# A new hand-written step order for a fused linear-attention and feed-forward kernel

## The chip, the cores and the metric

One core of a Trainium2 chip runs the whole kernel. The metric is the device time of one execution in microseconds. Before the change it is 151.06 us, the median of three runs (150.97 to 152.73).

The core has five engines that run side by side, each with its own queue of instructions that it works off strictly in order: TensorE (PE: matmuls, with PEld for loading weights into its array), VectorE (DVE), ScalarE (ACT), GpSimd (POOL) and SyncE (SP, which here only issues DMAs; ACT issues a few as well). Engines wait for each other through semaphores. An instruction that waits holds up everything behind it on its own engine.

## The reference, cut to what matters

```
xn  = layernorm(x)                                   # x: 2048 rows of 448, bf16
q, k, v = split(xn @ wqkv)                           # 16 heads of 28
phi(a)  = concat(softmax(a @ w_phi), softmax(-a @ w_phi))     # per head, 28 -> 56
kv = phi(k)^T v ;  z = sum of phi(k) over the rows   # over all 2048 rows
o  = (phi(q) kv) / (phi(q) z + 1e-6)
h  = xn @ w1 + b1                                    # 448 -> 1792
out = x + o @ wo + (h * tanh(softplus(h))) @ w2      # Mish in the middle
```

Because kv and z are sums over all rows, no row of the attention output can be made before every row's k and v have been.

## The kernel before, in words

**Tiling.** The 2048 rows are 16 tiles of 128 (t = 0 to 15), worked on in 8 pairs (u = 0 to 7, tiles 2u and 2u+1). Everything in bf16 stays in SBUF. PSUM is eight banks, used as four pairs of banks; a pair of row tiles or a feed-forward step holds one such bank pair from its first matmul until its result has been moved out.

**Where the order comes from.** There is no loop nest that decides the order. Every piece of work is a named step, a closure in a dictionary `steps`, and one string, `ORDER` (L147 on), lists the 298 names; `run_order` calls them one after the other:

```
def run_order(steps, order):
    for name in order:
        steps[name]()
```

Calling a step appends its instructions to the queues of the engines that it uses, so `ORDER` fixes the order within each of the five queues at once, and also which bank each step gets (the least recently used free one). Waits between engines are worked out from what each instruction reads and writes. Most steps exist in variants; the last letter says which engine does the work.

**The steps by name** (u a pair, t a tile, c a chunk of 128 rows of a weight):

- `lx0 lx1 lx2 lx3 lx4 lx6` load x: tiles 0-1, 2-3, 4-5, 6-7, 8-11, 12-15 (L270). `lkm`, `lvm` load the first 384 rows of the k and v weights, `lkt` their last 64 rows, twice (L273, L281). `lqT0..3` load the q weights transposed (L285). `lp`, `lb`, `lo`, `l2` load w_phi, b1, wo, w2; `l1m0..2` load chunks of W1 (L277), `l1t` its last 64 rows, twice (L281). A final `s` means issued by SP, `a` by ACT. `table` loads the ACT table for exp and ln (L315).
- `pi pm pw pv pk pp0 pp1 pp2` are set-up work on POOL (identity, masks, zeros, ones); `bd` builds the block-diagonal w_phi (L544). `z12` is twelve 128x512 matmuls on constants whose result nobody reads (L376).
- `st{t}` layernorm statistics of a tile: `d` on DVE (BATCH_NORM_STATS2 and an aggregate, L467, L468), `a` on ACT (copy with a sum, a small multiply, square with a sum). `rs{u}` makes 1/sqrt(var): `p` on POOL (L473, L476), `a` on ACT for both tiles at once, `t` on ACT tile by tile (L480, L482). `xn{u}` normalizes a pair: `d` on DVE (L501), `p` on POOL (L496) after a small DVE step (L489).
- `xt{u}` transposes the normalized pair into `xnT`: `m` by a DMA transpose that SP issues (L521), `a` or `d` by seven PE transposes (L509) moved out of PSUM by ACT or DVE, `b` the same with the move split, three blocks on ACT and four on DVE. A DMA transpose (but for pair 1) also waits for the loads of the first and the last tiles of x.
- `wtk{c}`, `wmk{c}`, `wmq{c}` fold w_phi into the k and q weights: PE transposes of the k weights (L556), then 112-row matmuls (L571); the last letter is the engine that moves the result out (L514 on ACT, L516 on DVE).
- `v{u}1 v{u}2`, `k{u}1 k{u}2`, `q{u}1 q{u}2` are the projections of a pair, each in two parts of 8 and 6 matmuls (L438) which work in the two 64-row halves of the array side by side. After part 2 of k and q, ACT makes the two exponentials (L600, L661); v is moved out by ACT (`a`) or DVE (`d`).
- `kn{u}.{s}` normalizes phi(k): a row sum and a reciprocal on DVE (L608, L610), the multiplication on POOL (L612). `kv{u}` adds a pair to kv and z on PE (L629). `kvz` moves kv out on DVE (L641) and transposes it by DMA.
- `e{t}` transposes phi(q) of a tile by DMA (L669). `nd{t}` makes numerator and denominator on PE (L703) and divides on DVE (L718 to L729). `ot{u}m` transposes the attention output by DMA (L738).
- `f{q}.{fc}{part}` is the first feed-forward matmul for half the rows (q = 0, 1) and 128 of the 1792 features (L438, 64x512 operands), in parts of 8 and 6 matmuls, then Mish on ACT (L680).
- `wo{u}`, `G{u}` and `g{t}` add the two output products (L843, L805, L821), DVE adds x (L770), `sto`, `stt` store (L861, L858).

**Order around the start in the queues before.** SP: lx3, lkm, lkt, lx2, lqT2, lqT1, lqT0, lqT3, lx6, lx0, lx4, l1t, xt2m, l1m2, l1m0, xt7m, ... PE: z12, wtk2, wtk0, wtk1, wmk2, xt3, wtk3, wmk0, wmk1, wmk3, v31, b1, v32, k31, ... ACT: lp, table, lx1, lb, lvm, rs3, the moves of wtk2 and wtk1, ...

Of the kernel before, what the change touches and what calls it, by code (L numbers as in the profile page):

```python
# [144 lines left out]


ORDER = """  # L147
lpa pp2 lx3s pm z12 st6d pi lkms table st7d pw lx1a lkts lba lvma bd rs3t wtk2a xn3d lx2s lqT2 wtk0d st3d pv wtk1a wmk2a
xt3a wtk3d lqT1 wmk0a wmk1a st2d wmk3a st5d v31d rs1p lqT0 st4d xn1d rs2p lqT3 b1 qd lx6s v32a k31 lx0s wmq1a lx4s pp1
wmq0a xn2p l1ts xt1d st14d st15d wmq2a wmq3a k32 k11 st12d rs7p st9d q11 xt2m st8d k12 st10d xn7d q31 rs4p v11d pp0 q12  # L150
xn4p st11d v12d q21 rs5p st13d q32 q22 xn5p k21 st0d l1m2s l1m0s rs6p xt7m v21d k22 st1d v22a ep e3 rs0p v71a pk xt4m
k71 v72a kn3.1 xn6d k72 xt5m k41 xn0d kn3.0 e2 xt6m xt0m v41d e5 k42 l1m1s v42d e4 q41 v51d q42 e6 e8 v52a kn2.0 k61
v61d k62 kn4.0 k01 k51 kn7.0 kn4.1 k02 v62d q51 k52 q52 kn0.0 e7 q61 e9 v01d q62 e12 kn1.1 kn6.1 e10 f0.11 e11 kn1.0
v02d f0.12 kn0.1 f1.01 f0.21 f1.02 f1.21 kn7.1 f1.31 f1.22 los kn2.1 q71 f1.32 f1.51 kn5.0 f0.22 e13 f1.52 q01 q72 q02
f0.61 l2s kn6.0 kv3 kv1 e15 kv2 kn5.1 kv4 kv6 e14 kv7 kv0 kv5 kvz f0.62 f0.71 f0.91 f1.81 f0.72 e1 f1.82 f0.121 f1.111
f0.122 f0.81 f0.92 f1.112 f0.82 f1.91 f0.131 f1.92 e0 nd2 f0.132 f0.31 f0.101 f0.32 nd0 f0.111 f0.102 f0.112 nd1 f1.71
f1.61 f1.72 f0.51 nd3 f1.62 f0.52 f1.41 f1.11 f0.01 f1.12 f0.41 f1.42 ot0m nd5 f0.42 f0.02 wo01 f1.131 f1.101 ot1m nd6
f1.132 G01 nd4 f1.102 G11 ot2m wob nd7 ot3m G02 wo02 f1.121 nd12 G12 f1.122 wo11 nd11 wo22 G31 wo31 nd10 wo12 G21 nd13
ot5m ot6m wo21 wo32 G62 nd8 G22 wo52 G32 nd9 ot4m wo61 G51 nd15 G61 nd14 wo51 G41 wo62 sto6 sto1 wo41 G52 ot7m g14 sto5
wo7F sto2 G42 wo7H sto0 wo42 g15 stt14 sto3 sto4 stt15  # L160
"""


# [824 lines left out]
```

## Time and profile before

| what | value |
| --- | --- |
| median of three runs | 151.06 us (150.97, 151.06, 152.73) |
| the profiled execution's own time | 150.35 us |
| its span, first to last instruction | 148.3 us |
| mean granted TensorE clock | 0.999 |
| busy: DVE, ACT, POOL | 100.7, 72.0, 44.4 us |
| HBM read, written | 7.02 MB, 1.84 MB |

The profile is one execution. Its span runs from the first to the last instruction; the execution's own time is 2.05 us longer, for what lies around the instructions. Times in a timeline are from the span's start. In a timeline row stand the start, the time to the end of the last instruction, the engine, the line, the operation, output and input, and how many instructions were merged; brackets give the idle time before and what ended it. The ends of matmuls are modelled and contain the latency of the array, so the steady pace of matmuls is read from the distance between starts.

### The profile page before, as it was taken

To read this page: it belongs to the slowest core of one execution; us is meant where nothing else is said; L and a number is where in the kernel's file an instruction comes from. 1 tells how busy PE (TensorE), PEld (TensorE's weight loads), DVE (VectorE), ACT (ScalarE), POOL (GpSimd) and SP (SyncE) were. 2 spreads that over 40 slices of the span, in tenths; PEclk is the share of its full clock that TensorE was granted. 3 is DMA by queue.
4 is the path that set the end of the run, shared out by engine and by line. 5 is a ranking of instruction groups with operands and counts; after the bars stand their busy time and mean duration, and the time that the engine had idled before them with its cause. 6 is when DMAs were issued, how large, how long until landed. Compare 5 with 4: busy or idle time off the path is not lost.

```text
span 148.3 us, 3988 instructions
## 1 busy us (share of the span) xinstructions
PE 143.7 (97%) x1731; PEld 75.9 (51%) x1731; DVE 100.7 (68%) x225; ACT 72.0 (49%) x83; POOL 44.4 (30%) x65
## 2 busy tenths in 40 slices
PE   7799999999999999999999999999999999999993
PEld 2456456556555475444454445555555555554452
DVE  0888889897999803003998278896789859983042
ACT  3589889978996899578566653202000000000000
POOL 5428489899899990000000000000000000000000
PEclk9999999999999999999999999999999999999999
DMA  5999998999939989960003300031003300306513
GB/s 123 301 190 346 182 275 130 163 205 256 139 67 174 242 242 267 210 113 0 0 4 62 62 4 0 21 73 34 4 2 66 62 0 4 62 4 186 186 52 134
DMA packets 39997, 17.24 MB, mean 116 GB/s; under 512 B 33964, under 2 KB 39212, under 8 KB 39980
## 3 DMA queue, kind: packets, MB, share of 16 engines
q1 hardware_dynamic: 38800, 16.29, 52.5%
q10 hardware_dynamic: 1180, 0.70, 1.9%
q8 instruction: 13, 0.21, 0.6%
q14 instruction: 4, 0.03, 0.1%
HBM read 7.02 MB, written 1.84 MB: 60 GB/s over the span
## 4 chain that ended last, share of the span: by engine, by line
PE 89%; DMA 6%; DVE 2%; issue 0%; ACT 0%; SPq 0%
PE PS L438 47%; PE PS L843 31%; PE PS L805 3%; DMA Wkv<-in_A_wqkv_dram 3%; DMA xnT<-xn 3%; PE PS L703 2%; PE PS L629 2%; PE PS L571 1%; PE PS L821 1%; DVE stats L467 1%; PE PS L556 1%; PE PS L509 1%; DVE xnT L516 0%; ACT Eq L514 0%; DVE x_all L770 0%
## 5 line engine op out<-in xcount | busy, mean ns | idle before, releaser
L438 PE MATMUL PS<-xnT,W 64*128 64x512 bf16 x392 | 44.8, 376 | 0.0
L680 ACT ACTIVATE actT<-PS,b1T 128x1024 bf16<-128x1024 f32 x28 | 30.1, 1112 | 24.3 <-PE PS L438 24.3
L843 PE MATMUL PS<-W,actT 64*128 64x448 bf16 x392 | 39.3, 349 | 0.0
L438 PEld LDWEIGHTS PS<-xnT,W 64*128 64x128 bf16 x392 | 18.8, 94 | 20.8 <-ACT actT L680 0.5
L843 PEld LDWEIGHTS PS<-W,actT 64*128 64x128 bf16 x392 | 18.1, 94 | 18.1 <-issue 0.3
L612 POOL TENSOR_TENSOR actT<-actT,rSk 128x896 bf16<-128x896 bf16 x16 | 26.6, 1702 | 0.7 <-DVE rSk L610 0.6
L770 DVE TENSOR_TENSOR x_all<-PS,x_all 128x448 bf16<-128x448 f32 (+1 forms) x16 | 9.2, 616 | 11.3 <-PE PS L821 5.6
L718 DVE COPY Sq<-PS 128x16 f32<-128x16 f32 x32 | 4.1, 169 | 18.6 <-PE PS L703 18.5
L608 DVE TENSOR_REDUCE Sk<-actT 128x32 f32<-128x896 bf16 x16 | 16.7, 1043 | 0.0
L600 ACT ACTIVATE actT<-PS 128x896 bf16<-128x896 f32 x16 | 13.8, 950 | 1.0 <-PE PS L438 0.9
L438 PE MATMUL PS<-Wkv,xnT 64*128 64x448 bf16 x112 | 13.2, 349 | 0.0
L438 PE MATMUL PS<-Wpq,xnT 64*128 64x448 bf16 x112 | 12.5, 349 | 0.4 <-DMA xnT<-xn 0.4
L467 DVE BATCH_NORM_STATS2 stats<-x_all 128x6 f32<-128x448 bf16 x16 | 9.7, 608 | 4.1 <-DMA x_all<-in_A_x_dram 4.1
L438 PE MATMUL PS<-Wpk,xnT 64*128 64x448 bf16 x112 | 12.5, 349 | 0.0
L726 DVE TENSOR_TENSOR v_all<-v_all 128x464 f32<-128x464 f32 x16 | 10.3, 642 | 0.6
L722 DVE TENSOR_TENSOR v_all<-PS,Sq 128x464 f32<-128x464 f32 x16 | 10.3, 642 | 0.5
L729 DVE TENSOR_TENSOR xn<-v_all,rden 128x448 bf16<-128x448 f32 x16 | 10.0, 625 | 0.6
L724 DVE TENSOR_TENSOR v_all<-PS,Sq 128x464 f32<-128x464 f32 x16 | 10.1, 631 | 0.0
L661 ACT ACTIVATE actT<-PS 128x896 bf16<-128x896 f32 x10 | 8.6, 921 | 1.1 <-PE PS L438 1.1
L438 PEld LDWEIGHTS PS<-Wpq,xnT 64*128 64x128 bf16 x112 | 5.9, 94 | 5.4 <-issue 0.8
L438 PEld LDWEIGHTS PS<-Wpk,xnT 64*128 64x128 bf16 x112 | 6.0, 94 | 4.4
L438 PEld LDWEIGHTS PS<-Wkv,xnT 64*128 64x128 bf16 x112 | 6.0, 94 | 4.3
(82 smaller groups left out, 126.4 us busy)
## 6 DMA issues: line engine op xcount, KB each, us to landing
W<-in_B_w_dram SPq DMA_DIRECT2D x1, 1568.0 KB, 10.1
out_dram<-x_all SPq DMA_DIRECT2D x7, 224.0 KB, 2.1
W<-in_B_w_dram SPq DMA_DIRECT2D x3, 448.0 KB, 4.1
x_all<-in_A_x_dram SPq DMA_DIRECT2D x2, 448.0 KB, 4.9
x_all<-in_A_x_dram SPq DMA_DIRECT2D x3, 224.0 KB, 3.8
Wo<-in_A_wo_dram SPq DMA_DIRECT2D x2, 336.0 KB, 4.1
W<-in_B_w_dram SPq DMA_DIRECT2D x2, 224.0 KB, 6.4
Wkv<-in_A_wqkv_dram SPq DMA_DIRECT2D x1, 336.0 KB, 4.5
```

The source lines that it names most:

```text
L438: ins = e.matmul(o, lhs(c, k), rhs(c, k), start=part == "1" and c == 0, stop=part == "2" and c == 2)
L467: op("DVE", lambda e: e.bn_stats(stats[:, t, :], x_all[:, t, :]), r=[("x", t)], w=[("st", t)], tag=f"bn{t}")
L600: op("ACT", lambda e, s=s: e.activation(E_of(u)[:, s, :, :], two(b, D), ACT.Exp, scale=1.0 if s == 0 else -1.0), r=[pb(b), pb(b + 1)], w=[ ...
L608: op("DVE", lambda e: e.tensor_reduce(Sk[u][:, s, :], Eh(), AX.X, ALU.add), r=[("E", u, s)], w=[("Sk", u, s)], tag=f"Sk{u}.{s}")
L612: op("POOL", lambda e: e.tensor_tensor(Eh(), Eh(), ap_on(rSk[u][:, s, 0:1], [[1, 2 * H], [0, DH]]), ALU.mult), r=[("E", u, s), ("rSk", u, ...
L680: op("ACT", lambda e: e.activation(actT[:, fc, q * 1024:(q + 1) * 1024], bank(b, 2), ACT.Mish, bias=b1T[:, fc:fc + 1]), r=[("b1T",), pb(b) ...
L722: op("DVE", lambda e: e.tensor_tensor(tv(t1[i]), num(0), sx(1), ALU.mult), r=[pb(b), pb(b + 1), ("Sq", i, 1)], w=[("t1", i)], tag=f"ta{t}")
L724: op("DVE", lambda e: e.tensor_tensor(tv(t2), num(1), sx(0), ALU.mult), r=[pb(b), pb(b + 1), ("Sq", i, 0)], w=[("t2",)], tag=f"tb{t}")
L726: op("DVE", lambda e: e.tensor_tensor(t1[i], t1[i], t2, ALU.add), r=[("t1", i), ("t2",)], w=[("t1", i)], tag=f"tc{t}")
L729: op("DVE", lambda e: e.tensor_tensor(o_sb[(t // 2) % 2][:, t % 2, :].rearrange("p (h d) -> p h d", d=DH), t1[i][:, :, 0:DH], ap_on(rden[i ...
L770: op("DVE", lambda e: e.tensor_tensor(x_all[:, t, 0:n], bank(b)[:, 0:n], x_all[:, t, 0:n], ALU.add), r=[pb(b), ("x", t)], w=[("out", t)], ...
L843: ins = e.matmul(bank(places[par][0])[:, 0:D], l, r, start=fresh[par], stop=places[par][2] and i >= len(todo) - 2)
```

## The change

Only the string `ORDER` changes: the same kernel functions, another sequence and other variants of some steps.

- The loads on SP up to `lx4` keep their queue and their order, and so do those on ACT. The two loads of W1's tail (`l1ts`) go from before `xt2m` to behind `e2`, so that of the loads only Wo and W2 still follow. W2's load goes from SP (`l2s`) to ACT (`l2a`).
- `z12` becomes `z16`: four more matmuls on constants ahead of the first weight transpose.
- On ACT `table` goes behind the four DMA issues. The statistics of tile 7 (`st7`), and 1/sqrt(var) of pairs 0, 1 and 5, go to ACT; pair 3's is made for both tiles at once.
- Pairs 0, 1 and 7 are normalized on POOL, 4 and 5 on DVE (before: 4 and 5 on POOL; 0, 1 and 7 on DVE). The transposes of pairs 1 and 3 are moved out by ACT and DVE together. wtk1 and wmq2 go from ACT to DVE. v is moved out of PSUM by ACT for pairs 1, 3, 4, 5, 6 and by DVE for 0, 2, 7 (before: ACT for 2, 3, 5, 7 and DVE for 0, 1, 4, 6).
- POOL's set-up (`pk`, `pp1`, `pp2`, `pw`) moves ahead of the identity, `pv` behind the last 1/sqrt(var).
- The two multiplications per pair of `kn`, the projections, feed-forward steps and output steps come in a new sequence. In each queue the number of matmuls is the same but for the four constants.

```
-lpa pp2 lx3s pm z12 st6d pi lkms table st7d pw lx1a lkts lba lvma bd rs3t wtk2a xn3d lx2s lqT2 wtk0d st3d pv wtk1a wmk2a
-xt3a wtk3d lqT1 wmk0a wmk1a st2d wmk3a st5d v31d rs1p lqT0 st4d xn1d rs2p lqT3 b1 qd lx6s v32a k31 lx0s wmq1a lx4s pp1
-wmq0a xn2p l1ts xt1d st14d st15d wmq2a wmq3a k32 k11 st12d rs7p st9d q11 xt2m st8d k12 st10d xn7d q31 rs4p v11d pp0 q12
-xn4p st11d v12d q21 rs5p st13d q32 q22 xn5p k21 st0d l1m2s l1m0s rs6p xt7m v21d k22 st1d v22a ep e3 rs0p v71a pk xt4m
-k71 v72a kn3.1 xn6d k72 xt5m k41 xn0d kn3.0 e2 xt6m xt0m v41d e5 k42 l1m1s v42d e4 q41 v51d q42 e6 e8 v52a kn2.0 k61
-v61d k62 kn4.0 k01 k51 kn7.0 kn4.1 k02 v62d q51 k52 q52 kn0.0 e7 q61 e9 v01d q62 e12 kn1.1 kn6.1 e10 f0.11 e11 kn1.0
-v02d f0.12 kn0.1 f1.01 f0.21 f1.02 f1.21 kn7.1 f1.31 f1.22 los kn2.1 q71 f1.32 f1.51 kn5.0 f0.22 e13 f1.52 q01 q72 q02
-f0.61 l2s kn6.0 kv3 kv1 e15 kv2 kn5.1 kv4 kv6 e14 kv7 kv0 kv5 kvz f0.62 f0.71 f0.91 f1.81 f0.72 e1 f1.82 f0.121 f1.111
...
+lpa lx1a lba lvma lx3s lkms lkts lx2s lqT2 lqT1 lqT0 lqT3 lx6s lx0s lx4s pk table pp1 pp2 pw st6d st7a st3d z16 pi st2d
+rs3a xn3d wtk2a wtk0d pm rs1a bd xn1p wtk1d b1 wmk2a xt3b wmk0a wtk3d wmk1a v31a st4d st5d rs2p wmk3a xt1b v32a qd pp0
+xn2p k11 xt2m wmq2d wmq1a st15d st14d ep wmq0a st13d wmq3a rs7p k12 st12d k31 q31 xn7p k32 st1d q32 q11 st9d v11d st8d
+q12 v12a k21 v21d st11d l1m2s xt7m st10d rs4p xn4d rs5a k22 rs6p l1m0s xt4m xn6d pv v22d xn5d q21 kn1.1 st0d k71 q22 k72
+v71a xt6m k41 v72d rs0a xn0p v41a k42 xt5m v42a l1m1s kn7.1 e3 e5 e4 k61 v51a xt0m kn2.1 kn1.0 k62 kn6.0 kn4.0 v52a k51
+e2 q51 l1ts k52 e6 q52 q41 e7 v61a v01a kn3.1 v62a kn3.0 q42 k01 v02d k02 q61 f1.31 q62 kn0.0 f0.11 e9 f1.32 kn0.1 f1.01
+f1.21 f1.02 f1.22 q71 e8 f0.12 q72 q01 kn2.0 e11 e12 f1.51 f0.21 kn7.0 e10 e13 q02 kn5.1 los f1.52 f0.22 kn4.1 kn6.1 kv3
+e1 kv0 kv4 kv2 kv6 kn5.0 kv1 kv7 kv5 kvz f0.31 f1.91 f0.32 f0.51 f0.91 e14 f1.92 f1.81 f0.92 f0.81 f0.52 f0.82 f1.111 e0
+e15 f1.82 f1.11 f1.112 nd1 f1.12 f0.01 nd0 f0.61 f1.71 f0.62 f1.72 l2a f0.111 f0.101 f0.112 f0.02 f0.71 f0.102 nd2 f0.72
+f0.41 nd3 f1.121 wob f0.42 ot0m f0.131 f1.122 f1.101 f0.132 ot1m nd4 f0.121 f1.102 nd5 f1.61 f0.122 f1.62 f1.41 ot2m nd7
+nd6 f1.42 G01 G11 G31 nd13 G02 f1.131 wo01 ot3m wo31 f1.132 G12 wo02 wo32 nd12 wo11 wo22 wo12 G32 nd10 G21 nd11 wo21
+sto3 G61 ot6m ot5m wo61 nd8 G41 nd9 G22 ot4m nd14 sto1 sto2 G62 G51 nd15 sto0 ot7m wo41 wo62 G42 wo51 wo42 wo52 g14 wo7F
+G52 sto4 sto6 wo7H g15 sto5 stt14 stt15
```

More of the change, by code (lines that the diff above doesn't have):

```diff
@@ L153 @@
-v61d k62 kn4.0 k01 k51 kn7.0 kn4.1 k02 v62d q51 k52 q52 kn0.0 e7 q61 e9 v01d q62 e12 kn1.1 kn6.1 e10 f0.11 e11 kn1.0
-v02d f0.12 kn0.1 f1.01 f0.21 f1.02 f1.21 kn7.1 f1.31 f1.22 los kn2.1 q71 f1.32 f1.51 kn5.0 f0.22 e13 f1.52 q01 q72 q02
-f0.61 l2s kn6.0 kv3 kv1 e15 kv2 kn5.1 kv4 kv6 e14 kv7 kv0 kv5 kvz f0.62 f0.71 f0.91 f1.81 f0.72 e1 f1.82 f0.121 f1.111
-f0.122 f0.81 f0.92 f1.112 f0.82 f1.91 f0.131 f1.92 e0 nd2 f0.132 f0.31 f0.101 f0.32 nd0 f0.111 f0.102 f0.112 nd1 f1.71
-f1.61 f1.72 f0.51 nd3 f1.62 f0.52 f1.41 f1.11 f0.01 f1.12 f0.41 f1.42 ot0m nd5 f0.42 f0.02 wo01 f1.131 f1.101 ot1m nd6
@@ L158 @@
-f1.132 G01 nd4 f1.102 G11 ot2m wob nd7 ot3m G02 wo02 f1.121 nd12 G12 f1.122 wo11 nd11 wo22 G31 wo31 nd10 wo12 G21 nd13
-ot5m ot6m wo21 wo32 G62 nd8 G22 wo52 G32 nd9 ot4m wo61 G51 nd15 G61 nd14 wo51 G41 wo62 sto6 sto1 wo41 G52 ot7m g14 sto5
-wo7F sto2 G42 wo7H sto0 wo42 g15 stt14 sto3 sto4 stt15
+lpa lx1a lba lvma lx3s lkms lkts lx2s lqT2 lqT1 lqT0 lqT3 lx6s lx0s lx4s pk table pp1 pp2 pw st6d st7a st3d z16 pi st2d
+rs3a xn3d wtk2a wtk0d pm rs1a bd xn1p wtk1d b1 wmk2a xt3b wmk0a wtk3d wmk1a v31a st4d st5d rs2p wmk3a xt1b v32a qd pp0
```

## The prediction

> **What bounds the kernel now.** I read the stretches first: the span cut where the matmuls change character, with the busy time and count of PE, PEld, DVE, ACT and POOL, then granted clock, DMA share and GB/s.
>
> ```profile
> 0.00:5.94 5.94, 4.65 (x12) 1.61 (x13) 2.09 (x6) 2.28 (x5) 3.54 (x16) 1.00 0.74 189
> 5.94:18.64 12.70, 11.85 (x141) 7.05 (x142) 10.73 (x34) 10.78 (x18) 5.92 (x13) 1.00 1.03 248
> 18.64:53.12 34.48, 34.48 (x351) 19.23 (x352) 30.44 (x57) 30.49 (x34) 32.56 (x34) 1.00 1.01 178
> 53.12:56.38 3.26, 3.26 (x130) 3.18 (x128) 0.00 (x0) 3.25 (x5) 2.42 (x4) 1.00 1.12 335
> 56.38:145.36 88.98, 88.98 (x1093) 44.48 (x1090) 56.67 (x129) 25.15 (x24) 0.00 (x0) 1.00 0.28 62
> 145.36:148.30 2.94, 0.51 (x18) 0.39 (x14) 0.75 (x2) 0.00 (x0) 0.00 (x0) 0.96 0.24 77
> ```
>
> PE is busy for 34.48 of 34.48, 3.26 of 3.26 and 88.98 of 88.98 us: from 18.64 to 145.36, 85% of the span, it has no gap. The change removes none of that work, so it can win only ahead of 18.64 and behind 145.36. The tail of 2.94 us is the last eviction and store, and both orders end in the same steps (half of pair 7's output product, `g15`, the split store). The first 5.94 us wait for k's weights, whose loads keep queue and place. That leaves 5.94 to 18.64, and PE's waits all lie there:
>
> ```profile
> PE PS L556 <- DMA Wkv<-in_A_wqkv_dram: 0.4, 1, 0.4
> PE PS L438 <- DMA xnT<-xn: 0.4, 1, 0.4
> PE PS L571 <- ACT Eq L514: 0.3, 1, 0.3
> ```
>
> They sum to 1.1 us, but ends of matmuls are modelled, so I take the holes from the starts in PE's timeline:
>
> ```profile
> 0.85 4.65 PE L376 MATMUL PS<-const-bfloat16-1.0 128*128 128x512 bf16 x12 [0.85 <-PEq L973]
> 5.94 0.85 PE L556 MATMUL PS<-ident,Wkv 128*112 128x128 bf16 x12 [0.44 <-DMA Wkv<-in_A_wqkv_dram]
> 7.12 0.36 PE L571 MATMUL PS<-Wbd,Eq 112*128 112x112 bf16 x4 [0.33 <-ACT Eq L514]
> 11.49 0.57 PE L571 MATMUL PS<-Wbd,WqT 112*128 112x112 bf16 x8
> 11.89 0.56 PE L509 MATMUL PS<-ident,xn 128*128 128x128 bf16 x7
> 12.29 0.56 PE L571 MATMUL PS<-Wbd,WqT 112*128 112x112 bf16 x8
> 16.95 0.73 PE L438 MATMUL PS<-Wpq,xnT 64*128 64x448 bf16 x6
> 17.52 0.73 PE L438 MATMUL PS<-Wkv,xnT 64*128 64x448 bf16 x6
> 18.64 1.69 PE L438 MATMUL PS<-Wpq,xnT 64*128 64x448 bf16 x16 [0.40 <-DMA xnT<-xn]
> ```
>
> Paces: six projection matmuls go from 16.95 to 17.52 (0.095 each), eight small ones from 11.49 to 11.89 (0.05), seven transposes from 11.89 to 12.29 (0.057). The 141 matmuls of the stretch are 78, 32 and 30 of these and the bias transpose (0.1): 7.4 + 1.6 + 1.7 + 0.1 = 10.8 us in 12.70. So the holes are 1.9 us, and this is the **ceiling of any gain**: 1.3% of the time. One hole is plain: the six from 17.52 need 0.57 too, and the next starts 1.12 later, 0.55 lost to the DMA transpose of pair 2.
>
> **The change, part by part.**
>
> *Warm-up.* Twelve constant matmuls become sixteen. The last rows of that group:
>
> ```profile
> 4.90 0.60 PE L376 MATMUL PS<-const-bfloat16-1.0 128*128 128x512 bf16 x2
> 5.12 0.38 PE L376 MATMUL PS<-const-bfloat16-1.0 128*128 128x512 bf16 x1
> ```
>
> The last two start 0.22 apart. Four more put the last start at 5.12 + 0.88 = 6.00 and free PE at 6.22, where k's weights let it go on at 5.94. Price: +0.28 at that place.
>
> *Early chain.* These rows set it:
>
> ```profile
> 1.27 1.28 ACT L315 ACT_TABLE_LOAD   x1 [1.27 <-PEq L973]
> 1.30 0.48 ACTq L270 DMA_DIRECT2D x_all<-in_A_x_dram  x1
> 2.50 0.41 ACTq L273 DMA_DIRECT2D Wkv<-in_A_wqkv_dram  x1
> 4.61 0.29 ACT L480 ACTIVATE lnv<-mv,eps_col 128x1 f32<-128x1 f32 x1 [2.06 <-DVE mv L468]
> 4.93 0.20 ACT L482 ACTIVATE rstd<-lnv 128x1 f32<-128x1 f32 x1
> 6.38 1.08 ACT L514 ACTIVATE Eq<-PS 112x512 bf16<-112x512 bf16 x2 [0.60 <-PE PS L556]
> x_all<-in_A_x_dram ACTq DMA_DIRECT2D x1, 224.0 KB, 4.1
> 6.60 0.42 DVE L516 COPY Eq<-PS 112x512 bf16<-112x512 bf16 x1 [0.21 <-PE PS L556]
> 10.10 0.60 DVE L467 BATCH_NORM_STATS2 stats<-x_all 128x6 f32<-128x448 bf16 x1
> 10.83 0.86 DVE L501 TENSOR_SCALAR xn<-x_all,mv,rstd 128x448 bf16<-128x448 bf16 x3
> 12.45 1.74 POOL L496 TENSOR_SCALAR xn<-x_all,rstd,shift 128x448 bf16<-128x448 bf16 x3
> ```
>
> The table load runs beside the DMA issues (1.27 and 1.30), so moving it behind them brings x no earlier: tiles 2-3 still land at 1.30 + 4.1 = 5.4. It now runs at 2.9 to 4.2. Then ACT makes tile 7's statistics, which no row shows on ACT. Nearest are a plain move (0.54 each for the two of 512 columns at 6.38) for its two passes over 448 columns and the small 4.61 and 4.93 rows for the multiply: 0.54 + 0.25 + 0.54, about 1.4, which I take; half of that and 2.4 (the passes at double price, for the sum that they carry) are the ends. 1/sqrt(var) adds 0.5 (0.29 + 0.20): ready at 6.1, between 5.4 and 7.1. DVE does tiles 3 and 2 meanwhile (one every 0.73, 10.10 to 10.83): 5.4 to 6.95. So pair 3 is normalized from 6.95 to 7.8 (0.86), and DVE's own statistics hide ACT's; without that cover ACT's upper end would cost 0.15.
>
> PE: wtk2 at 6.22; its eviction and wmk2 as before 1.18 later (5.94 to 7.12), 7.40; xt3 at 7.9, not at 7.3, since DVE is later; wmk0 8.3, wtk3, wmk1 8.85 behind DVE's evictions (0.42 each); v31 at 9.2. POOL normalizes pair 1 in 1.74 from 8.3, so xt1 runs at 10.3. k11 waits for both halves of its eviction, ACT's behind wmk3's and DVE's behind two statistics, until 11.65 (0.4 idle). From there the projections and the four wmq run closed up but for 0.1: k12 ends at 13.9, q31 starts 14.7, v12 ends at **19.27**. Before, the same work and `q32` would be done at 18.64 + 0.57 = 19.21. So 13.27 us from 5.94 become 13.05 from 6.22: 0.28 lost at the start, 0.22 won in holes (0.55 at pair 2's transpose, less 0.33 more in the waits for xt3 and k11): **+0.06 us**. The bounds: -0.9 if the waits for xt3, v31 and k11 (0.35, 0.15, 0.4) are covered; +0.6 if each small DVE and ACT eviction is one 0.42 to 0.54 later.
>
> *W1's tails.* They are two DMAs ahead of pair 2's transpose:
>
> ```profile
> 10.34 1.12 SPq L281 DMA_DIRECT2D W<-in_B_w_dram  x2
> 14.22 1.26 SPq L521 DMA_TRANSPOSE xnT<-xn  x1
> DMA to landing us min/median/max: 3.0/3.5/4.3
> W<-in_B_w_dram SPq DMA_DIRECT2D x2, 224.0 KB, 6.4
> W<-in_B_w_dram SPq DMA_DIRECT2D x1, 1568.0 KB, 10.1
> ```
>
> The issue at 14.22 is POOL's doing (12.45 + 1.74), and POOL is no earlier now. It landed 4.3 later, the slowest of six; without the tails in front it lands 3.0 to 4.3 after issue, 17.2 to 18.5. Both are ahead of 19.27, because `q32` and the rest stand in front of `k21`: the tails' move itself is worth 0 to PE, the new sequence covers the stall either way. The tails now issue behind pair 0's transpose, which POOL releases at 29.9 (below), and `e2`, 1.3 each on SP: 32.6, and at 6.4 they land at 39. The first feed-forward step stands at 19.27 + 16 x 0.76 + 15 x 0.57 = 39.9 (the parts ahead of it). Cover 0.9; should SP be 1 us behind, 0.1 is paid. W2's load, at 10.1 us, issues from ACT after a Mish at some 73.5 (eleven feed-forward steps of 1.5 behind `kv`) and is needed at 89 (ten more): it is hidden.
>
> *Normalizing phi(k).* What is late next is POOL's chain towards `kv`:
>
> ```profile
> 28.00 9.98 POOL L612 TENSOR_TENSOR actT<-actT,rSk 128x896 bf16<-128x896 bf16 x6
> 38.62 16.61 POOL L612 TENSOR_TENSOR actT<-actT,rSk 128x896 bf16<-128x896 bf16 x10 [0.64 <-DVE rSk L610]
> 53.12 3.34 PE L629 MATMUL PS<-actT,v_all 128*60 128x112 bf16 x128
> ```
>
> Ten take 16.61, one each 1.66. Before, the chain ends at 55.23 and the eighth `kv` step starts at 53.12 + 7 x 0.39 = 55.9 (3.34, less some 0.2 of latency, for eight): 0.65 to spare. Now one of the sixteen goes early, then pair 0 is normalized on POOL, which needs DVE, which first moves out v of pair 7. That projection ends at 19.27 + 6 x 0.76 + 5 x 0.57 = 26.7; with 0.3 of latency and 1.1 for the move (an estimate, two of the 0.54 moves), POOL starts at 28.2 and ends at 29.9, and the chain at 29.9 + 15 x 1.66 = 54.9. `kv` starts at 52.3, since one feed-forward part of eight less stands ahead of it (8 x 0.107 = 0.86, an estimate at 512 columns for 448), and its last step at 55.05. **Slack 0.15**: price zero, but every further delay there is paid in full.
>
> *The rest* (moved feed-forward, output and store steps; same instructions): in the stretch from 56.38 ACT needs 1.05 per instruction (25.15 for 24) against 14 x 0.107 = 1.5 on PE for the feed-forward step that feeds it, and DVE is busy for 56.67 of 88.98, so PE stays the bound. Price 0, with at most 0.3 where a bank comes free late.
>
> The profiled execution took 150.35: 150.35 + 0.06 = 150.4. It lies 0.7 below the median of the runs, 151.06, so I expect **151.1 us**.
>
> **Two rules of the skill.** In the warm-up the first ten of twelve start between 0.85 and 4.90, 0.41 apart, the last two 0.22, while the granted clock reads 1.00 throughout. The Trainium skill (TensorE: Matmul & The Clock Gate, section "What's actually happening") says that the array runs at half pace until a free-running window has seen it busy, so the number of slow matmuls changes from run to run; the trace agrees on the halving, a second phase is not in it.
> The fetches that the order is scored over are thirteen packets:
>
> ```profile
> q8 instruction: 13, 0.21, 0.6%
> ```
>
> They reach to the end of the span, and PE has no gap from 18.64 on, so I see nothing there to win. The Trainium skill (Runtime: NRT & Kernel Launch, section "Instruction fetch mechanics") says that the sequencer fetches the next page while it runs the present one, mostly hidden; the trace agrees, and by it the sum has no term for fetches.
>
> **Rivals.**
> *Faster, 150.2* (0.16): the waits for xt3, v31 and k11 are covered, -0.9. For: PE, DVE and ACT all have idle time in 5.94 to 18.64 (10.73 and 10.78 busy of 12.70). Against: then `kv` stands against POOL's chain, which caps the gain at 0.15 plus what the chain gains itself.
> *Slower, 152.3* (0.20): POOL's chain decides. If pair 0's normalization starts more than 0.15 late, PE stands idle ahead of the last `kv`. Place: v of pair 7 queued on DVE, pair 0's statistics and shift behind it. Late by one such move (1.1) and the slack, the last `kv` waits some 1.2: 151.1 + 1.2. For: the slack of 0.15 is the end of a long sum, half of it estimates. Against: the chain rests on PE's own progress, so both slip together.
> *Slow start, 151.7* (0.09): the warm-up's fast pace comes later, after fourteen slow matmuls instead of ten. Then PE is free at 0.85 + 14 x 0.42 + 2 x 0.22 = 7.2; the wait for xt3 absorbs half of the extra 1.0: +0.6. Against: the one trace shows the pace change at 4.6. (The clock-gate page named above has this as its rule.)
> *It does what it says and nothing follows*: that is my forecast, 151.1 (0.55), with its own spread of 150.6 to 151.7.
>
> **How the numbers follow.** 2%, about what a measurement of this kernel can tell from no change, is 3.0 us. The ceiling of 1.9 us keeps any gain inside it: faster 0.01. Slower by 3.0 us needs POOL's chain late by twice an eviction and an early stall as well: 0.04. Same 0.95. The range holds the forecast, most of the faster case and the slower one: 150.1 to 152.5.
>
> **What would show it.** Right: PE without a gap behind some 19 us but for at most 0.3 ahead of the last `kv`; first weight transpose at 6.2; no wait of `k21` for a transpose; POOL's last multiplication ending at 54.5 to 55.5. Wrong: first weight transpose at 5.94 although sixteen run ahead; PE waiting for POOL, for W1's tails or for bank pairs; a stretch from 56 on that is longer than 89 us.

## The result, and the profile after

On the chip that timed both, the kernel before took 150.64 us (median of 22 runs, 150.07 to 152.73) and the changed one 151.94 (22 runs, 150.84 to 155.32). The ratio is **1.0082, with a 95% interval of 1.0057 to 1.0108**: the change costs some 0.8%, about 1.2 us. That is inside the forecast's range (150.1 to 152.5) and inside its "within 2%"; the forecast of 151.1 itself was 0.84 too low, and since before ran here at 150.64 and not at 151.06, the change's own share was missed by about 1.2 us.

In 3 of the 22 runs the mean granted clock is 0.989, and in the profiled one of them (154.52) matmuls run at half pace for some 3.5 us behind a stall; such runs are left out of all ratios and of the medians from here on (151.93 without them), and the sums below are made with a second profile of the same kernel, which lacks that stretch (152.82, span 151.1 against 148.3 of before). That second profile is of a long execution: the runs taken with it go down to 151.33. Its longest wait of PE, and the rows of PE's timeline that answer to those of before (start, time, engine, line, operation, count, idle time before):

```profile
PE PS L438 <- DMA xnT<-xn: 2.4, 1, 2.4
```
```profile
6.66 0.83 PE L556 MATMUL PS<-ident,Wkv 128*112 128x128 bf16 x12
...
8.01 0.56 PE L509 MATMUL PS<-ident,xn 128*128 128x128 bf16 x7
...
19.17 0.92 PE L438 MATMUL PS<-Wpk,xnT 64*128 64x448 bf16 x8
...
24.46 0.92 PE L438 MATMUL PS<-Wkv,xnT 64*128 64x448 bf16 x8
27.76 0.93 PE L438 MATMUL PS<-Wpk,xnT 64*128 64x448 bf16 x8 [2.38 <-DMA xnT<-xn]
```

The 0.4 for pair 2's transpose has vanished, and a new one stands far behind the place where the forecast saw the last gap. Eight matmuls need 0.76, so the eight from 24.46 are fed until 25.22, and `k41` starts at 27.76: a hole of **2.54 us**. It is the projection of pair 4, it waits for pair 4's DMA transpose, and the stretches show PE busy ahead of it and idle in it:

```profile
6.66:19.17 12.51, 12.25 (x150) 7.33 (x149) 10.84 (x38) 10.67 (x19) 7.43 (x15) 1.00 0.82 211
19.17:25.22 6.05, 6.05 (x66) 3.02 (x62) 5.95 (x16) 5.87 (x10) 2.38 (x5) 1.00 1.00 167
25.22:27.76 2.54, 0.16 (x2) 0.03 (x1) 0.97 (x3) 2.51 (x5) 1.70 (x1) 1.00 1.10 62
```

Columns: length, then busy time and count of PE, PEld, DVE, ACT, POOL, then granted clock, DMA share, GB/s. PE has 0.16 of 2.54 while the DMA engines read 1.10 busy and move 62 GB/s, a third of the 167 ahead of it. The last matmuls, 64 columns wide, start at these places in before and in this profile:

```profile
145.30 0.57 PE L787 MATMUL PS<-W,actT 128*128 128x64 bf16 x14
147.97 0.57 PE L787 MATMUL PS<-W,actT 128*128 128x64 bf16 x14
```

From the first weight transpose that is 145.30 - 5.94 = 139.36 before and 147.97 - 6.66 = 141.31 now. So the 2.7 us more of span are +0.72 at the start and +1.95 between (the new hole of 2.54 less pair 2's 0.55 comes to 1.99); the tail is the same within 0.1. The transposes of pair 4 in the two kernels, issue windows 21.5 to 21.6 of before and 21.2 to 21.4 of the second profile (count, then us from issue to landing):

```profile
xnT<-xn SPq DMA_TRANSPOSE x1, 3.0
```
```profile
xnT<-xn SPq DMA_TRANSPOSE x1, 6.4
```

The same transfer, issued at nearly the same time of the span (21.55 and 21.27), lands 3.0 us later in one kernel and 6.4 later in the other. That is the question of the study.

### The profile page after: what moved, and what is told of

Read it like the earlier page. It is cut to its first block, busy times and chain, and to the rows that moved or that the text cites. A ratio compares the mean times of both kernels' runs of the same rounds, so it can differ in the third digit from the quotient of the medians.

```text
span 152.8 us, 3996 instructions
## 1 busy us (share of the span) xinstructions
PE 146.8 (96%) x1735; PEld 77.7 (51%) x1735; DVE 98.7 (65%) x223; ACT 74.4 (49%) x92; POOL 43.3 (28%) x62
## 4 chain that ended last, share of the span: by engine, by line
PE 83%; DVE 7%; DMA 7%; issue 0%; ACTq 0%; DVEq 0%
PE PS L438 42%; PE PS L843 30%; DMA xnT<-xn 4%; DVE stats L467 4%; PE PS L805 3%; DMA x_all<-in_A_x_dram 3%; PE PS L703 2%; PE PS L629 2%; DVE mv L468 1%; DVE xn L501 1%; PE PS L821 1%; PE PS L509 1%; PE PS L571 1%; DVE Wpq L516 0%; DVE x_all L770 0%
## 5 line engine op out<-in xcount | busy, mean ns | idle before, releaser
L612 POOL TENSOR_TENSOR actT<-actT,rSk 128x896 bf16<-128x896 bf16 x16 | 26.7, 1699 | 5.8 <-DVE rSk L610 5.7
L438 PE MATMUL PS<-Wpk,xnT 64*128 64x448 bf16 x112 | 13.8, 361 | 2.1 <-DMA xnT<-xn 2.1
L438 PE MATMUL PS<-Wkv,xnT 64*128 64x448 bf16 x112 | 14.0, 374 | 0.0
L467 DVE BATCH_NORM_STATS2 stats<-x_all 128x6 f32<-128x448 bf16 x15 | 9.1, 604 | 5.0 <-DMA x_all<-in_A_x_dram 5.0
L726 DVE TENSOR_TENSOR v_all<-v_all 128x464 f32<-128x464 f32 x16 | 10.3, 643 | 0.6
L722 DVE TENSOR_TENSOR v_all<-PS,Sq 128x464 f32<-128x464 f32 x16 | 10.3, 641 | 0.5
L496 POOL TENSOR_SCALAR xn<-x_all,rstd,shift 128x448 bf16<-128x448 bf16 (+2 forms) x12 | 6.9, 589 | 6.6 <-DVE shift L489 6.5
```

The lines of the kernel that those rows point to most:

```text
L438: ins = e.matmul(o, lhs(c, k), rhs(c, k), start=part == "1" and c == 0, stop=part == "2" and c == 2)
L467: op("DVE", lambda e: e.bn_stats(stats[:, t, :], x_all[:, t, :]), r=[("x", t)], w=[("st", t)], tag=f"bn{t}")
L612: op("POOL", lambda e: e.tensor_tensor(Eh(), Eh(), ap_on(rSk[u][:, s, 0:1], [[1, 2 * H], [0, DH]]), ALU.mult), r=[("E", u, s), ("rSk", u, ...
L722: op("DVE", lambda e: e.tensor_tensor(tv(t1[i]), num(0), sx(1), ALU.mult), r=[pb(b), pb(b + 1), ("Sq", i, 1)], w=[("t1", i)], tag=f"ta{t}")
L726: op("DVE", lambda e: e.tensor_tensor(t1[i], t1[i], t2, ALU.add), r=[("t1", i), ("t2",)], w=[("t1", i)], tag=f"tc{t}")
```

## The experiments

Two theories of the late landing. **Fetch**: in both kernels a 16 KB packet of PE's own instructions is moved by the same DMA engines at about this time (the queue q8 of the forecast's row of thirteen packets), tied to how far PE has come in its instructions and not to the data; a transpose in flight at that moment is held up. (The count is not exact: in the fourteen profiles 439 to 471 weight loads and matmuls are recorded ahead of this packet.) **Queue**: W1's second chunk (`l1m0s`, 448 KB) now stands in SP's queue between the transposes of pairs 7 and 4, where before it stood ahead of both, and simply delays pair 4's. As windows of a tenth of a microsecond around the packet show (before, then the second profile), it is there in both, and longer in the changed kernel; the share is of 16 engines, so 58.2% of 0.1 us is 0.93 us of one engine and 130.5% is 2.09:

```profile
q8 instruction: 1, 0.02, 58.2%
```
```profile
q8 instruction: 1, 0.02, 130.5%
```

The same view of the second profile from 22 to 29:

```profile
DMA  3889893999939999601049000010109999999990
GB/s 143 328 348 369 348 416 124 240 247 218 92 54 290 348 239 155 29 7 7 7 89 123 0 0 0 6 9 9 10 15 139 230 287 276 288 293 287 530 123 0
```

In these two rows each of 40 slices is 0.175 us. Behind 24.3 (slice 13) the rate falls twice, to 7 to 29 GB/s and then to 0 to 15: the transpose is not slow for lack of bandwidth, it stands still. The zeros of the DMA row do not mean idle engines: this view books all of a packet's time in the slice in which the packet starts. In the trace 19 to 25 packets are in flight all through 24.6 to 27.2, some of 256 bytes for 0.7 to 1.5 us, where 0.02 to 0.05 is usual. In before, the transpose's data were through at about 24.0, just ahead of the packet at 24.64.

### The changed kernel again, and without its four extra constants

> The changed kernel again, as the measure for the others. All theories: 151.9 us, a wait of k41 for pair 4's DMA transpose of 0 to 2.3 us, and where it is long a stretch of PE at half pace behind it.

151.96 us (6 runs, 151.33 to 152.82; ratio 1.0100, 1.0067 to 1.0133). The profile is the second one of above, with its wait of 2.4 us.

```
-pp1 pp2 pw st6d st7a st3d z16 pi st2d
+pp1 pp2 pw st6d st7a st3d z12 pi st2d
```

> Twelve constant matmuls instead of sixteen, all else as changed. Theory fetch: PE's second instruction page is asked for 8 instructions later, some 0.4 us, when pair 4's transpose is nearly through; the wait of k41 shrinks below 0.5 and the time falls by 0.8 or more, to 151.1 or less. Theory queue: the wait stays at its length, 151.6 to 151.9. Theory warm-up (the start is what costs): 0.3 less, 151.6, and the wait stays.

151.76 us (8 runs; ratio 1.0072, 1.0034 to 1.0109). In PE's stream the packet now comes eight instructions (four weight loads, four matmuls) later. The wait, and the landing (issue window 21.6 to 21.8):

```profile
PE PS L438 <- DVE stats L467: 0.6, 1, 0.6
```
```profile
xnT<-xn SPq DMA_TRANSPOSE x1, 4.6
```

The packet now comes at 26.50, behind the landing (21.71 + 4.6 = 26.3), and the wait is 0.6 for 2.4. (The releaser named, DVE's statistics, had long been done; `k41` starts 0.14 behind the landing.) That is 2.1 us later than in the second profile and not the 0.4 expected; part of it is that PE itself stands waiting up to 26.46. The time did not come down as expected (151.1 or less), and the interval of its ratio overlaps that of the changed kernel. What is left of the delay goes with the chunk, which still stands directly ahead, and with a smaller packet (below).

### Twelve constants and four of one column

The same as the last, but with four matmuls of one column behind the twelve. They cost 0.2 us in a place where PE waits for weights anyway, and put PE's packet back to the instruction where it was. Wait, landing (issue window 21.0 to 21.2) and packet (24.0 to 24.1) stand below.

```
+            for _ in range(small):
+                ins = e.matmul(bank(b)[:, 0:1], ap_on(one, [[0, P]]), ap_on(one, [[0, 1]]), start=True, stop=True)
-... st3d z16 pi st2d
+... st3d z12s4 pi st2d
```

> Twelve constant matmuls and four of one column, so that the count of instructions, and with it the place of the page fetch, is that of the changed kernel, while the warm-up is short as before. Theory fetch: the wait of k41 is as in the changed kernel, 151.7 to 151.9. Theory queue: the same. Theory warm-up: 151.6. Against the kernel with twelve alone: fetch expects it slower by 0.5 or more, the other two equal.

```profile
PE PS L440 <- DMA xnT<-xn: 2.2, 1, 2.2
```
```profile
xnT<-xn SPq DMA_TRANSPOSE x1, 6.2
q8 instruction: 1, 0.02, 123.4%
```

With the packet back in the transfer (at 24.05, 1.98 us long) the wait is back at 2.2. (The granted clock is 1.00 up to the end of that wait.) The queues of DMAs are identical in the two kernels, so for these two executions the **queue alone cannot be the cause**, and the fetch is part of it. The times do not bear it out: 151.60 us (7 runs; ratio 1.0068, 1.0040 to 1.0097) beside 151.76 of the last kernel, where the fetch theory expected 0.5 more. A profile is one execution, and the place of the packet against the data changes with each.

### Fifty-six instructions earlier

Twelve constants and 32 of one column: PE's packet should come ahead of pair 4's transpose instead of into it.

```
-... st3d z16 pi st2d
+... st3d z12s32 pi st2d
```

> Twelve constant matmuls and thirty-two of one column in place of sixteen: 56 instructions more ahead of the work, so PE's second page is asked for some 2.6 us earlier, at about 22, in the plain copy of l1m0 and not in a transpose; the warm-up ends no later than with sixteen. Theory fetch: the wait of k41 falls to 0.3 to 1.0 (the other engines' smaller page fetch at 24.2 stays), no half pace, 151.2 or less. Theory queue: the wait stays at 2.1 to 2.4, 151.9 to 152.7.

```profile
PE PS L440 <- DVE mv L470: 0.9, 1, 0.9
```
```profile
xnT<-xn SPq DMA_TRANSPOSE x1, 4.9
```

151.72 us (6 runs; ratio 1.0083, 1.0053 to 1.0112). PE's packet is at 21.30, at the transpose's issue, and the wait is 0.9: less than half, but not gone, and the chunk is still ahead. The queue theory had the wait unchanged. The time again did not follow: 151.2 or less was expected, and the ratio is that of the changed kernel.

### W1's second chunk elsewhere

First behind pair 5's transpose, then straight behind the first chunk, ahead of pair 7's transpose:

```
-k22 rs6p l1m0s xt4m xn6d ... k42 xt5m v42a
+k22 rs6p xt4m xn6d ... k42 xt5m l1m0s v42a
```

> One load moved: the chunk l1m0 of W1 goes from ahead of pair 4's transpose on SP to behind pair 5's. Both theories (the queue ahead of the transpose makes it late; the instruction page fetched in the middle of it makes it late) expect it to land by 24.8 instead of 27.65, no wait of k41, and 1.0 us less than the changed kernel: 150.9. If the wait stays, both are wrong.

```
-st11d l1m2s xt7m ... k22 rs6p l1m0s xt4m xn6d
+st11d l1m2s l1m0s xt7m ... k22 rs6p xt4m xn6d
```

> The changed kernel with the W1 chunk l1m0 back where it was before, directly behind l1m2 and ahead of pair 7's transpose. Theory fetch: pair 4's transpose is through the rings some 0.9 us earlier, by about 24.5, at or ahead of the page fetches at 24.2 to 24.6; the wait of k41 falls from 2.1 to 2.4 to 0.5 or less, nothing runs at half pace, 150.6 to 151.0. Theory queue: the same, since the chunk no longer stands ahead. If the wait stays above 1.5, the chunk has no part in it.

Waits of the first, then waits and landing of the second:

```profile
PE PS L438 <- DVE mv L468: 0.8, 1, 0.8
PE PS L438 <- ACT actT L600: 0.5, 1, 0.5
```
```profile
PE PS L438 <- DVE mv L468: 0.9, 1, 0.9
```
```profile
xnT<-xn SPq DMA_TRANSPOSE x1, 4.8
```

The first gave 153.08 us (6 runs; ratio 1.0159, 1.0123 to 1.0194), against my expectation of a gain: the wait at `k41` falls to 0.8 (landing 4.8 behind issue, the packet at 24.54 still inside), but k's weights came late in this profile (first weight transpose at 6.79), and new waits on ACT stand further on (holes between starts of 0.73 and 0.38 at the feed-forward steps `f1.31` and `f1.21`, 0.27 at `q71`). I put these down to both chunks of W1 standing ahead of the transposes of phi(q) now, which no run shows by itself. The second gave 151.34 (12 runs; ratio 1.0056, 1.0027 to 1.0085): wait 0.9, nothing new behind it. By the waits the chunk in the queue does its part too; the ratios of the changed kernel and of this one still overlap.

The counterpart in the order of before, with the chunk put directly ahead of pair 4's transpose:

```
-st0d l1m2s l1m0s rs6p xt7m ... ep e3 rs0p v71a pk xt4m
+st0d l1m2s rs6p xt7m ... ep e3 l1m0s rs0p v71a pk xt4m
```

> The other way round: the kernel before, with l1m0 moved to directly ahead of pair 4's transpose. There k41 starts at 25.8 and the transpose landed at 24.5. Theory fetch: the transpose is still in the rings at the page fetch (24.6) and lands at 26.5 to 27.5; k41 waits 0.7 to 1.7 us, 151.2 to 152.2. Theory queue: it lands 0.9 later, at 25.4, and no wait is seen, 150.5.

```profile
PE PS L438 <- DMA xnT<-xn: 2.8, 1, 2.8
```
```profile
xnT<-xn SPq DMA_TRANSPOSE x1, 5.9
```

152.64 us (5 runs, 150.69 to 152.72; ratio 1.0109, 1.0068 to 1.0149; not among them the profiled one, 153.59): in the profile one step moved in the old order makes as large a wait as the whole change. It is larger than the 0.7 to 1.7 that I expected, because the issue itself slid by 1.5 us, to 23.03 (0.5 of it a later start), and the packet at 26.72 then met the transfer.

### Before, with the packet moved

The order of before, changed only in the number of constants: sixteen of 512 columns, or twelve and sixteen of one column.

```
-lpa pp2 lx3s pm z12 st6d
+lpa pp2 lx3s pm z16 st6d
```

> The order of before with sixteen constant matmuls of 512 columns in the warm-up instead of twelve; everything else is the same. The forecast's term is +0.28 us at the start, of which waits behind it may take back some: 150.5 to 150.8 beside 150.5 of before. Fetch theory: PE's second instruction fetch comes four matmuls (eight instructions, some 0.3 to 0.4 us) earlier in the order and the order itself starts 0.0 to 0.3 us later, so that it falls at 24.3 to 24.6, upon or ahead of the last data of pair 4's transpose; where it meets that data, the landing is at 25.5 or later, against 24.5, and k41 (at 25.8 in before) waits up to 1 us.

> The order of before, with sixteen extra constant matmuls of one column behind the twelve of the warm-up. DMA queues, issues and all other steps are those of before. The extra matmuls are done ahead of the arrival of k's weights and cost nothing there. Fetch theory: PE's second instruction fetch moves forward by 32 instructions, some 1.5 us, to about 23.2 us, in the middle of the transfer of pair 4's transpose: that transpose lands at 25.5 to 27 instead of 24.5, k41 waits up to 1 us for it, and the time is 0 to 1 us above that of before. Theory that the queue alone makes the transpose late: the landing stays at 24.5 and the time at that of before.

PE's rows of the first, and the landing of both (issue windows 22.0 to 22.2 and 21.7 to 21.9):

```profile
0.85 6.57 PE L376 MATMUL PS<-const-bfloat16-1.0 128*128 128x512 bf16 x16 [0.85 <-PEq L973]
7.26 0.83 PE L556 MATMUL PS<-ident,Wkv 128*112 128x128 bf16 x12
...
25.86 0.73 PE L438 MATMUL PS<-Wpk,xnT 64*128 64x448 bf16 x6
26.92 0.93 PE L438 MATMUL PS<-Wpk,xnT 64*128 64x448 bf16 x8 [0.32 <-DMA xnT<-xn]
```
```profile
xnT<-xn SPq DMA_TRANSPOSE x1, 4.7
```
```profile
xnT<-xn SPq DMA_TRANSPOSE x1, 4.5
```

151.06 us (10 runs; ratio 1.0038, 1.0013 to 1.0063) and 151.14 (6 runs; 1.0061, 1.0040 to 1.0081). With no DMA moved at all, the transpose that took 3.0 us takes 4.7 and 4.5, and `k41` has holes of 0.49 and 0.31 that before does not have. The packets are at 24.66 and 24.29, 2.6 and 2.5 behind the issue instead of 3.1. The fetch theory holds in the kernel before as well, and the trace shows how. A DMA transpose reports its landing in 16 parts. In the kernel with sixteen of one column 15 of them come at 24.61 to 24.73, 2.9 us behind the issue as in before, and the last alone at 26.28; the packet ran from 24.28 to 25.24. In the one with sixteen of 512 columns all 16 come at 26.7, although of the 32 packets of 4 bytes that close the transpose 30 had started by 24.65; the other two start at 25.8, behind the instruction packet, which ran from 24.67 to 25.61. (In the second I had put the packet at 23.2; it came at 24.29, since the order itself started 0.4 later.) The sixteen constants show a second cost, below.

### The tails of W1 alone

```
-wmq0a xn2p l1ts xt1d ... kn3.0 e2 xt6m xt0m
+wmq0a xn2p xt1d ... kn3.0 e2 l1ts xt6m xt0m
```

> The order of before with one step moved: the two tails of W1 are issued behind pair 0's partner step e2, and no longer ahead of pair 1's work. The forecast put the worth of this alone at the stall of pair 2's transpose, 0.55 us of hole in before. Theory of the forecast: that hole goes, PE's wait for xnT at that place is 0 to 0.1, and the time is 0.3 to 0.5 below that of before (150.0 to 150.2), if everything behind has no other bound. Rival, fetch theory: PE now comes 0.5 us earlier to pair 4's transpose and to its second instruction fetch, which is tied to the count of PE's instructions; the transpose of pair 4 keeps its place in SP's queue and so loses its lead of some 0.1 us over the fetch: it lands 1 to 2 us later than in before, k41 waits 0.5 to 1.5 us and the time is that of before or up to 1 us more.

```profile
17.69 0.73 PE L438 MATMUL PS<-Wkv,xnT 64*128 64x448 bf16 x6
18.25 2.06 PE L438 MATMUL PS<-Wpq,xnT 64*128 64x448 bf16 x20
...
30.17 0.73 PE L438 MATMUL PS<-Wkv,xnT 64*128 64x448 bf16 x6
32.16 0.93 PE L438 MATMUL PS<-Wpk,xnT 64*128 64x448 bf16 x8 [1.26 <-ACT actT L661]
```

151.57 us (6 runs; ratio 1.0091, 1.0067 to 1.0114). The hole of pair 2 is gone, as the forecast had it (six from 17.69, the next at 18.25), and everything up to 30.17 is that much earlier; then `k61` waits 1.4, as the tails now stand in the queue ahead of pair 6's transpose. It is issued at 28.14 for 26.72 in before and lands at 32.02 for 30.34. Both theories missed this: pair 4 landed at 24.05, ahead of the packet at 24.72, since SP too was 0.44 us earlier. In the changed kernel that place is harmless, because all eight transposes stand ahead of the tails.

### Pair 4 without a DMA

The transpose of pair 4 on PE, moved out by DVE, in the changed kernel:

```
-k22 rs6p l1m0s xt4m xn6d
+k22 rs6p l1m0s xt4d xn6d
```

> The changed kernel, pair 4 transposed on TensorE and moved out by DVE in place of the DMA transpose. Theory fetch and theory queue: no wait of k41 for a DMA; PE pays 0.4 for seven transposes and DVE 0.6; 150.8 to 151.3, 0.7 or more below the changed kernel, and no run with PE at half pace. If it stays at 151.9 or more, the wait was not what costs.

```profile
PE PS L438 <- ACT actT L600: 0.7, 1, 0.7
```

152.25 us (6 runs; ratio 1.0111, 1.0094 to 1.0128). No wait for a DMA is left, but the seven transposes take a pair of banks and 0.5 us of PE, and `k71` now waits 0.7 for ACT to empty a bank. By the expectation's own sign (151.9 or more) this speaks against the wait as the cost. The profiled execution, with 151.52 the fastest of the six, fits a wait traded for a smaller one; what holds the other five at 152.1 to 152.3 no profile shows.

### Mended

Three edits at once: twelve constants, the chunk straight behind the first, and `k41` behind the move of v of pair 7, an edit that no run tries alone.

```
-st3d z16 pi ... st11d l1m2s xt7m ... rs6p l1m0s xt4m ... xt6m k41 v72d rs0a
+st3d z12 pi ... st11d l1m2s l1m0s xt7m ... rs6p xt4m ... xt6m v72d k41 rs0a
```

> The changed kernel with three steps put elsewhere: twelve constant matmuls instead of sixteen, W1's second chunk issued straight behind the first (ahead of pair 7's transpose and not ahead of pair 4's), and the projection k41 behind the eviction of v of pair 7. Theory: pair 4's transpose is no longer queued behind that chunk and the matmuls are counted further ahead of the fetch; k41's wait is at most 0.5 us instead of 2.1 to 2.4, and the time is 150.4 to 150.8, that of before. Rival: the wait for pair 4's transpose was never the whole of the loss (the later first steps, and POOL's chain that has no slack, hold the time): then it stays at 151.3 or above.

The landing (issue window 20.8 to 21.0), and rows of the timelines of PE and POOL:

```profile
xnT<-xn SPq DMA_TRANSPOSE x1, 3.8
```
```profile
6.01 0.85 PE L556 MATMUL PS<-ident,Wkv 128*112 128x128 bf16 x12
...
25.68 0.54 PE L438 MATMUL PS<-Wpk,xnT 64*128 64x448 bf16 x4
52.24 3.34 PE L629 MATMUL PS<-actT,v_all 128*60 128x112 bf16 x128
145.32 0.57 PE L787 MATMUL PS<-W,actT 128*128 128x64 bf16 x14
```
```profile
49.91 5.01 POOL L612 TENSOR_TENSOR actT<-actT,rSk 128x896 bf16<-128x896 bf16 x3
```

150.88 us (12 runs, 150.17 to 151.33; ratio **1.0025**, 1.0001 to 1.0049; before 150.39 on that chip): 0.6 to 0.75% below the changed kernel's ratios, though a shade above before and 0.1 above what I expected. The transpose lands 3.8 behind its issue, at 24.7, and the packet comes at 25.02; `k41` stands at 25.68, 0.24 behind the end of what precedes it, and no wait is named there. From the first weight transpose to the last narrow matmuls it takes 145.32 - 6.01 = 139.31, against 139.36 of before and 141.31 of the second profile. It is the only version whose interval lies clear of the changed kernel's; 0.65 of the gain in the profiles is the earlier start (6.01 for 6.66), the rest the wait. No version beats before.

### The runs side by side

Pair 4's transpose, in each profile: when SP issued it, when PE's packet was moved and how long it took, how long the transpose took to land, and PE's wait for it.

| kernel | issue | PE's packet | issue to landing | wait at `k41` |
| --- | --- | --- | --- | --- |
| before | 21.55 | 24.64, 0.93 | 3.0 | none |
| before, 16 constants | 22.10 | 24.66, 0.94 | 4.7 | 0.3 |
| before, 16 of one column | 21.78 | 24.29, 0.96 | 4.5 | 0.3 (hole) |
| before, chunk ahead | 23.03 | 26.72, 0.93 | 5.9 | 2.8 |
| changed, first profile | 21.57 | 24.56, 2.13 | 6.1 | 2.1 |
| changed, second | 21.27 | 24.36, 2.09 | 6.4 | 2.4 |
| 12 constants | 21.71 | 26.50, 1.03 | 4.6 | 0.6 |
| 12 and 4 of one column | 21.12 | 24.05, 1.98 | 6.2 | 2.2 |
| 12 and 32 of one column | 21.35 | 21.30, 1.40 | 4.9 | 0.9 |
| chunk behind pair 5 | 22.04 | 24.54, 1.48 | 4.8 | 0.8 |
| chunk behind the first | 21.06 | 23.87, 1.21 | 4.8 | 0.9 |
| mended | 20.92 | 25.02, 1.07 | 3.8 | none |

Sorted by the two theories, the landing takes 3.0 and 3.8 us with neither (before, mended); **4.5 to 4.8 with PE's packet inside the transfer and no chunk directly ahead** (four kernels); 4.6 to 4.9 with the chunk directly ahead and PE's packet outside (12, and 12 and 32); and 5.9 to 6.4 with both (four profiles). The orders leave some 4 us between issue and need, so the middle groups make PE wait for 0.3 to 0.9 and the last for 2.1 to 2.8.

This sorting leaves out a third thing that the traces show: smaller packets of instructions, 8 KB each, of another queue, q14. In before they come at 26.70 and 28.38, behind pair 4's landing. In the changed kernel, with other work on DVE, ACT and POOL, they come at 23.02 and 24.22 (second profile), inside the transfer. In the mended one a q14 packet at 23.30, which took 0.85, is the only one inside (window 23.25 to 23.35):

```profile
q14 instruction: 1, 0.01, 53.2%
```

Nine of the 16 parts of its landing come by 23.81, 2.9 behind the issue, and seven at 24.7, behind the packet: that is its 3.8 for 3.0. In the two kernels with the chunk ahead and PE's packet outside a q14 packet lies inside as well (24.78 and 24.76), and the landing comes at 26.3. So **the chunk alone was not measured**. What can be read for it is the first data of pair 4: 1.8 to 2.0 us behind the issue with the chunk directly ahead in the changed orders, 1.2 without, which makes it some 0.6 to 0.8 us.

Taken over all fourteen profiles, 83 DMA transposes of a pair were issued. In 40 no packet of q8 or q14 starts between issue and landing, and they took 2.9 to 3.9 us. In the other 43 one does; 31 of these took 4.0 or more, up to 6.4. (A longer transfer also has more time for one to fall into, so this alone would not prove which is the cause; the held parts do.)

## Why the prediction was right and where it was wrong

*The walk through the start: right in its steps, its end by luck.* It put the first weight transpose at 6.22, xn of pair 3 at 6.95 to 7.8, the transpose xt3 at 7.9, v31 at 9.2, xt1 at 10.3, and v12's end, from a start at 6.22, at 19.27. In the second profile, which starts 0.44 later at 6.66, the last four stand at 8.01, 9.19, 10.26 and 19.17, and xn of pair 3 at 6.93. So the walk took 12.51 us for the 13.05 forecast, and a start 0.44 too late made up for it. ACT's rows:

```profile
4.24 0.58 ACT L459 ACTIVATE junk<-x_all 128x448 bf16<-128x448 bf16 x1
4.72 0.19 ACT L459 ACTIVATION_READ_ACCUMULATOR junk<-x_all 128x1 f32 x1
4.94 0.20 ACT L461 ACTIVATE rmean<-mv 128x1 f32<-128x1 f32 x1
5.18 0.67 ACT L463 ACTIVATE junk<-x_all,rmean 128x448 bf16<-128x448 bf16 x1
5.75 0.19 ACT L463 ACTIVATION_READ_ACCUMULATOR junk<-x_all,rmean 128x1 f32 x1
```

The statistics of a tile on ACT took 4.24 to 5.94, 1.7 us where 1.4 was taken and 2.4 was the bound: the two passes cost 0.58 and 0.67, the multiply between them 0.20, and each pass is followed by a row of 0.19 that reads the accumulator, which the term lacked. DVE's own statistics covered it, as said. The table load did move to 2.95 without any effect on x.

*Pair 2's transpose and W1's tails: right in the time, the cause doubtful.* The 0.55 us hole is gone and the tails cost nothing in this order (they landed at 39.3 and 40.4 in the first profile, and no wait names them). Put there in the old order, they cost 1.4 at pair 6. But the forecast tied the slow landing of pair 2's transpose, 4.3, to the tails ahead of it. With the tails still ahead it took 2.9 and 3.0 in the two kernels of before with more constants. It was slow in two profiles only, before and before with the chunk moved (4.3 and 4.0), and in these two PE's first packet starts in the middle of it. In before (issue at 14.22, window 15.4 to 15.5):

```profile
q8 instruction: 1, 0.02, 73.0%
```

That is 1.17 us from 15.47 on. The other slow transpose of before, pair 5's, issued at 23.87 and also 4.3, has PE's second packet in it (24.64). Whether the tails made the first packet come late (it comes at 13.69 in the run without them) is open.

*The sixteen constants: mis-sized.* +0.28 came from one profile, in which the last of twelve already ran at the full pace. The pace changes at another moment in each run: sixteen took 4.92 to 6.57 us in these profiles. In the run of before with sixteen, all sixteen were slow and the first weight transpose stood at 7.26 for 5.94: up to +1.3, and the time went up by 0.4% (1.0013 to 1.0063), part of it the 0.5 of `k41`. k's weights vary as well (first weight transpose at 6.20 to 6.42 in three of the profiles with twelve). Five of the six profiles with sixteen have their first weight transpose behind 6.22 (6.44 to 7.26, one of them waiting for k's weights), so the rival **Slow start** (0.09) was underrated.

*POOL's chain: right.* The mended kernel, without the stall, has `kv` at 52.24 and the end of the chain at 49.91 + 5.01 = 54.92; the forecast had 52.3 and 54.9. The last `kv` step starts at 52.24 + 7 x 0.39 = 54.97. The forecast's slack of 0.15 (its own terms, 29.9 + 15 x 1.66, give 54.8 and 0.25) measures 0.05 there, and was not overdrawn. The rival **Slower**, 152.3, came nearer to the time than the forecast and had the wrong mechanism: no row of the changed kernel's two profiles shows PE waiting for POOL.

*"PE without a gap behind some 19 us", and "the sum has no term for fetches": wrong.* This is the step that failed. I costed the wait of pair 2's transpose alone and took the six transposes of 3.0 to 4.3 as covered, because PE had no gap behind 18.64 before. Three things were not in the working: that pair 4's was issued at 21.55, landed at 24.55 and was needed by 25.83, a margin of 1.3; that `l1m0s`, moved past pair 7's transpose, stands directly ahead of pair 4's now (issued at 20.24 in the first profile) and takes some 0.6 to 0.8 of it; and that a packet of instructions which meets a transpose costs it 0.8 to 1.8 us (3.8, and 4.5 to 4.8, for 3.0). The Trainium skill (Runtime: NRT & Kernel Launch, section "Instruction fetch mechanics") has the next page fetched during the present one and the cost mostly hidden; for PE the traces agree, no row behind the start shows it waiting for instructions. The conclusion that I drew, no term, does not follow: the packet costs the transfers beside it. The rows for it lay in the trace of before, where of the six transposes the two that took 4.3 are the two with PE's packet in them.

The total came out inside the range by luck: the missing term is small beside 3.0 us, 2%, and the range was wide enough for a rival of another mechanism. In the second profile: start +0.72 (foreseen 0.28), pair 2's hole -0.55 (foreseen), `k41` +2.54 (not foreseen), the rest about 0. The median moved by less, +1.3, so the typical unprofiled run probably waits less than these two profiles do; none was traced to show it. That the mended order gets back to 1.0025 says that all but a quarter of a per cent of the loss hangs on its three edits together. The kernels with a single edit (1.0056 to 1.0111, but for the chunk behind pair 5 at 1.0159) are not clear of the changed kernel's 1.0057 to 1.0108, so how the loss divides among the edits is read from profiles alone.

**What stays open.** Which engine the q14 packets belong to, and why other transfers in flight stand still with the held part, no run here shows; nor why the kernel with the packet back in place (12 and 4 of one column) is no slower in its ratio than the one with 12, although its profile waits 1.6 us more. The table rests on one profile for each kernel, two for the changed one.

## What to carry to other kernels

A stretch in which the bound engine never waits can be a stretch of thin covers: before an order is changed, list for every transfer in it when it is issued, when it lands and when it is needed, and charge each moved DMA to the transfers that it newly stands in front of. Instruction packets of all engines belong in that list, at about the place in the instructions where the trace of before has them: adding or taking away a few instructions far ahead, or moving work to another engine, can put them into another transfer. A "free" warm-up is free only as long as its slowest pace still ends ahead of the data.

## What the runs showed of the hardware

- A 16 KB packet of PE's instructions takes 0.9 to 1.5 us at this place in most of the profiles and 2.0 to 2.1 in three of the changed order. The transpose of pair 4 with it alone inside landed 4.5 and 4.7 us behind its issue (before with more constants) and not 3.0. PE itself does not wait for it.
- What comes late can be a few of the 16 parts of the transfer's landing: 1 of 16 in before with sixteen of one column (26.28, the others by 24.73), 5 of 16 with the chunk behind the first (25.9, the others by 23.93; there a q14 packet is inside as well). In before with sixteen of 512 columns it is all 16 (26.7).
- An 8 KB packet of q14 does the same on a smaller scale: 7 of 16 parts 0.9 us late in the mended kernel.
- The same load of k's weights, at the same place of the same queue, let PE start at 5.94 in the profile of before, at 6.42 in that of before with W1's chunk moved (identical up to there), and at 6.79 in one of the changed order.
